# 24 of the 32 V groups as two 64-row halves added by GpSimd, four attention A pieces moved into the loop, a new loop order

## The chip, the cores and the metric

One core of a Trainium2 chip. The time is the device time of one execution in microseconds (us); the kernel before took a median of 1776.0 us in three runs (1775.54 to 1776.98). The engines are TensorE (PE; its weight loads stand apart as PEld), VectorE (DVE), ScalarE (ACT), GpSimd (POOL) and SyncE (SP), which issues nearly all DMAs.

## What is computed

Two attentions of 32 heads of 20 over 2048 positions, side by side in the output:

```python
# A: each position sees 8 positions, 2 apart, ending at itself
logits = einsum("bhsd,bhswd->bhsw", q, kg) * scale      # kg, vg: gathered k and v
o_a = einsum("bhsw,bhswd->bhsd", softmax(where(mask, logits, -1e9)), vg)
# B: full attention
p = softmax(einsum("bhqd,bhkd->bhqk", q, k) * Dh**-0.5)
o_b = einsum("bhqk,bhkd->bhqd", p, v)
return concatenate([o_a @ wo_a, o_b @ wo_b], axis=-1)   # q, k, v from x @ wqkv, each its own
```

All in fp32. The projections split both operands in a high and a low part (type fp32r) and add three products: high x high, high x low, low x high (`PASSES`).

## The kernel before

**Stages.** First attention A's projections, then B's q and k (both stored in memory). Then the *V stage*, B's v. Then the *loop*: B's attention in 512 steps (488 in the loop, the last 24 in a tail), with A's attention on GpSimd beside it. Then the rest of the output.

**A V group** (`v_group`, L854) makes 128 positions x 320 columns of v: 15 matmuls (five chunks of 128 of the contraction, three products each; `rows15`, L250) that add up in one PSUM bank, `ww` the weights' tiles and `xn`, `xl` those of x. ACT copies the bank into `ve`, one of four tiles (`ones`) that already hold a one beside each head, and SP stores `ve` in `vb_d`. Of 32 groups 30 run in the V stage, two in the loop's first steps. Banks come from four that rotate (`bank`, `give`).

**Score sets in the V stage.** B's softmax needs row maxima before its exponentials. A set (`b_max`, L687) is four matmuls of 60 rows x 512 columns (`bk`, `bq`): two pairs, one of a pair on rows 0 to 63 and the other on rows 64 to 127 of the array, into two adjacent banks, then one DVE maximum over both banks (`mx`). The sets run 24 steps ahead of the loop (`LEAD`): after each V group from the seventh on, one set.

**Order.** Every engine runs its instructions in program order (`InOrder`). `after(n, ...)` puts something n ticks later, `tick()` ends one; a V group is a tick, a loop step is a tick. After groups 8 and 16, x is loaded and split again (ACT takes the high part, GpSimd subtracts, `x_pieces(xb, ..., gp)`).

**Attention A** is 128 pieces (`a_attention`, `a_unit`): a piece loads two tiles of k or v (`akv`), multiplies by q (`aq`) or by the probabilities (`al`), and adds up, all on GpSimd. Twelve pieces run beside B's q and k, four in the V stage (after groups 18, 24, 27 and 30), the others in the loop, where `begin` hands them out by an estimate of GpSimd's time.

**The loop's order** is written out in the string `ORDER` (L944). S is two score halves (half of a step's 62-row matmul on 64 array rows) and their exponentials on ACT; M and N are two halves of the row maxima, M with one DVE maximum over two banks, N with two over one bank each; Y is one half of each kind; V begins the next step with its product with v; F is an output group of A; j is one DVE transpose for A; the digits are PSUM banks.

Of the kernel before, what the change touches and what calls it, by code (L numbers as in the profile page):

```python
# [10 lines left out]
F32 = mybir.dt.float32  # L11
# [8 lines left out]
DH = 20  # L20
# [50 lines left out]
def attention_pair(ctx, tc, xa, wqk_a, wv_a, wo_a, xb, wqk_b, wv_b, wo_b, oa, ob):  # L71
# [104 lines left out]
    def chunk(t, xi, k):  # L176
        return t[k // (KC - 1)][:, xi, k % (KC - 1)]
# [739 lines left out]
    def begin(i):  # L917
# [32 lines left out]
        "Y07M5M2S41F0Y71M5S42Y03V7S42M5Y01VY24Y35S06N17V2S03M4Y16VY70S15M3Y26V7S05jS14jM2VjM5S01Y23V4jY05M6S31VN05M2M6"  # L950
        "S14jF0Y15S42M6Y03V1Y24M6S05VY02M3S57Y61V0Y72M3S56VY71M5S24Y30V1S27M5Y43VS07Y62N54N31F0Y72S36Y54N01V7Y62N34S05V"
        "Y06S51Y23N74V0S13M5Y72VS13N74Y56N20F1Y72S36M4Y01V7Y62M4S03VY06M1S35S74N60V3Y72S16M4VY70M1S64S35N07V6Y41S02Y53V"
        "M0S72Y34V5Y06S71N42VY07M3S61Y25V7Y60S14N32VY06S15M3Y27V6Y01M3S52VS70M1M3M5F7Y04S31Y25N76V0Y15N43S72VY71S26Y54"
        "N03V7S64M1Y05VS64S03jN21jY57jF6jjY70M1S35Y46V7Y05M1S34VY03M5S41S72N30V4Y57S36M1VY07M5S31S42N70V3Y41M5S72VY70M1"
        "S46Y35V0Y74S16M2VY71M4S63Y20V7Y61M4S32VY06M2S14S75N60V1Y72S36M4VS07M2S64N51V0S72Y36M4VS76M2S10M4S76Y32V1Y07M4"
        "S26VY07S23M4S61N70V2Y36S75Y14VM6S05Y43V1Y02S76N53VY07S24M5S31N70V2Y36M4S71VY07Y16M4M2Y70F1Y72S36M4Y01V7Y62M4"
        "S03VY06M1S35Y74V0Y35M1S76VS73Y45S62N10V7M3S51Y06VM3S52Y16V0jY75M3S26VjY71M5S24Y30V1Y27M5S43VY07M3jM5jS21jF0Y71"
        "M3S25Y06V7Y51M3S02VY06M1S53Y74V0Y35M1S76VY73M4S62Y10V7Y62M4S31VY06M2S14S75N60V1Y72S36M4VY07M2S64S51N70V6Y52M3"
        "S71VY70Y15S24M6S03N15V2S07Y64Y31VM4S07Y61V3Y02M4S71VS07Y62M4S13V0Y72S64N15VY71M2S46S50N17V4Y35S62M0VY73Y26M0M4"
        "Y37F2Y01S36M4Y72V0Y13M4S76VY71M2S64S05N17V6Y04M2S51VY70N15Y42S36V0Y17M3S56VY71S26M3Y50V1Y27S63M4VjS07jM2M4Y61"  # L960
        "F0jjjY72S13M4Y06V7Y13M4S02VS06M2S14N75V0S16M2Y74VS15M6S23N04V1Y27M5S03VS07M2Y46S51V0S72M3Y56VY71M3S25Y60Y17V2"
        "Y36M4S01VY07Y16M4S32Y70V1Y26M4S73VY07M2S64S51N70V6Y52M3S71VY70M1S53S46N07V5Y41M2S06VY70Y61M2S45S07V6M4Y31S02V"
        "S75M3S02N16V7Y05S41M2VY06M4Y13S72Y60V1S72M4Y36VY07M4M2S61F0Y71M2Y46S05V7Y04M2S15VY06M4S13Y72Y60V1Y75M3S26VY07"
        "M5S24Y31V0jS72jM5S43jVjM1S74Y56V3jY70M1S46VY07M4S61M2Y70F6Y70S15M2Y46V7Y05S13Y24VM0S63Y45V2Y01M6S35VY01M3S75"
        "Y62V0Y17M3S56VY75M1Y63S04V5Y67M1S04VY07M3S62S15N70V6Y14M2S75VY70M4S13S26N07V1Y25M3S06VY07M5S24S31N70V2Y36M4S71"
        "VY07S16N35S42N70V1S36M4Y72VS03M4M6Y21F0Y72S36M4Y01V7Y62M4S03VY06M1S35S74N60V3S72M5S41VY07M5S42V1Y07S34M5VY07"
        "S23M5Y41V7Y02M5S34VY03M1S46S57N30V4Y51M2S76VY70M5S13S42N07V1S63M4Y02VY73S04M5jY21jF7jjjY06S51M3Y72V0Y16M3S75V"
        "Y71M5S24S03N17V2Y06S15M3VY07M5S14Y32V7Y01M5S43VY04M1S35Y67V0Y53M1S46VS73M4S62N01V7S63M4Y02VS31Y06M4S72Y36V1Y07"
        "M4S26VY07M2S46Y51V7Y04M2S65VY06M4S13Y27Y60V1Y25M3S76VS07M5S24Y31V0Y72M5S41VY74M2S16S50N47V1Y26M4S03VY07M2S64"
        "S51N70V6Y52M3S71VY70M1S53S46N07V5S41M2Y06VY74M2M0S65F7Y62S35M0Y74V6Y53M0S72VY75M3S20Y16V7Y05M3S21VjS06jM1M3S57"  # L970
        "jF0jjY71S26M3Y05V7Y61M3S02VY06M1S53S74N60V5Y71S62M3VY07M1S63Y45V0Y76M1S34VY73M5S42Y10V7Y24M5S31VY04M2S15S76N40"
        "V1Y72S35N46VY07S25M3S61N07V2S36M4Y01VS73S04M5N12V7M5S03Y41VY02S36Y54N71V0S26M3Y75VS61M3S72Y05V6Y71M3S52VY70M1"
        "S53S46N07V5Y41M2S06VY70S61M2M4Y07F6Y70M2S14Y56V7Y04M2S15VY06M4S13Y72Y60V1Y75S24N36VY07S25M3Y61V7Y02M3S56VY05"
        "S61M3Y27V5Y60M3S12VS07M1S63jM4jF0jjjY71M4S63Y02V7Y61M4S03VY06M1S35Y74V0Y35M1S76VY73M4S62Y10V3Y76M4S21VY07M1S64"
        "Y53V0Y74M1S56VY73M4S62S01N37V6Y05M3S21VY70M1S53S46N07V5Y41M2S06VY70Y61M2S45Y07V6Y51M2S04VY70M4S13S26N07V1Y25M3"
        "S06VS07M5Y24S31V0S72M5Y43VM1S75S64N30V7Y61S52M3VY06M1S53S47N60V5Y41S23M6VY04M1S37M5N40F3Y72S16M4Y03V7Y62M4S01V"
        "Y06M2S14S75N60V1Y72S63M4VY07M2S64S51N70V6Y52M3S71VY70M1S53Y46V7Y05M1S34VjS06jM3M1S57jF0jjY71S26M3Y05V7Y61M3S02"
        "VS06M1S53Y74V0M1S65Y43VY71M5S23V4Y70S12M5VY70M1S36S54N70V3S21M5Y47VY02S14M5S73N02V1S74M5Y03VY72S06M4S31N72V0"
# [12 lines left out]
        "jjY71S26M3Y05V7Y61M3S02VY06M1S53Y74V0Y35M1S76VY73M4S62Y10V3Y76M4S21VY07M1S64Y53V7Y60M1S45VY06M4S31S27N60V3S24"
        "Y15M6VY02M4S17S63N02V1S74M5Y03VS72jM5S04Y31jV7jY06M1S54VjM5S03S42N17jS06S53N14V2Y01M6S54VY03S15Y74N62V3Y40S15"
# [113 lines left out]
```

## Time and profile before

| | us |
|---|---|
| median of 3 runs | 1776.0 |
| the profiled execution | 1777.45 |
| its span, first to last instruction | 1775.6 |
| DVE, ACT, POOL busy in the span | 1337.9, 1323.5, 1209.8 |
| span of the 32 `ve` copies | 351.5 to 446.6 |

A row of a group of instructions reads: line, engine, operation, tile written<-tiles read, shapes, count | busy us, mean ns of one | idle time of the engine before them and what ended it. All work goes through one helper, so every row has L66, and the tiles' names tell the groups apart. A timeline row begins with its start and its length in us. Matmul durations are modelled and overlap, so starts are compared rather than lengths.

### The profile page before, as it was taken

What the parts mean: (1) busy time and instruction counts of PE and PEld (TensorE: products, weight loads), DVE (VectorE), ACT (ScalarE), POOL (GpSimd) and SP (SyncE); (2) the same over time, 40 slices, a digit from 0 to 9 for tenths busy, and PEclk for the clock granted to TensorE, in tenths of its full rate; (3) what the DMA queues carried; (4) which work ended last, traced back from release to release, by engine and by line L of the source; (5) the groups of instructions that cost most, each with busy time, mean ns of one, the idle gap of its engine ahead of it and who ended that gap; (6) DMA issues with size and microseconds to landing.
All of it is one profiled execution on the core that took longest, in us unless ns stands there. A gap on an engine that the chain in (4) does not pass through costs nothing.

```text
span 1775.6 us, 31540 instructions
## 1 busy us (share of the span) xinstructions
PE 1760.9 (99%) x11211; PEld 996.6 (56%) x11211; DVE 1337.9 (75%) x1805; ACT 1323.5 (75%) x2593; POOL 1209.8 (68%) x1072
## 2 busy tenths in 40 slices
PE   9999999999999999999999999999999999999999
PEld 7988888887444444444444444444444444444569
DVE  3100232268999999999999999999999999999300
ACT  4222322222998999989999999999999998999881
POOL 0000059227899999999999999899999962445241
PEclk9999999999999999999999999999999999999999
DMA  6333596854744544364436436353644422211123
GB/s 229 112 98 109 177 309 243 277 175 145 221 120 123 147 137 124 107 159 150 133 104 173 134 114 160 111 156 117 163 127 121 139 68 51 72 40 47 33 71 114
DMA packets 191190, 240.22 MB, mean 135 GB/s; under 512 B 89020, under 2 KB 115260, under 8 KB 190040
## 3 DMA queue, kind: packets, MB, share of 16 engines
q1 hardware_dynamic: 190456, 237.54, 45.0%
q8 instruction: 88, 1.44, 0.3%
q14 instruction: 70, 0.57, 0.1%
q10 hardware_dynamic: 576, 0.66, 0.1%
HBM read 173.21 MB, written 64.91 MB: 134 GB/s over the span
## 4 chain that ended last, share of the span: by engine, by line
PE 77%; POOL 13%; DVE 3%; issue 2%; DMA 2%; ACT 2%; SPq 1%; POOLq 0%; ACTq 0%; DVEq 0%
PE ps_st L66 77%; POOL akv L66 7%; DVE mx L66 3%; POOL braw L66 3%; POOL ao L66 1%; ACT e L66 1%; SPq L66 1%; DMA bq<-qb_d 1%; POOL al L66 1%; DMA stg<-wv_b 0%; POOL aot L66 0%; DMA stg<-xa 0%; ACT more L66 0%; DMA ot_b<-braw 0%; DMA rb<-s_d 0%
## 5 line engine op out<-in xcount | busy, mean ns | idle before, releaser
L66 DVE TENSOR_REDUCE mx<-ps_st 128x1 f32<-128x512 f32 (+1 forms) x1483 | 1214.6, 884 | 46.3 <-PE ps_st L66 41.4
L66 ACT ACTIVATE e<-ps_st 128x512 f32<-128x512 f32 x2048 | 1063.3, 616 | 32.9 <-PE ps_st L66 12.9
L66 PE MATMUL ps_st<-bq,bk 62*128 62x512 f32 x2048 | 560.9, 440 | 2.9 <-DMA bq<-mdr 1.6
L66 PE MATMUL ps_st<-e,vb 128*32 128x512 f32 x4096 | 544.6, 606 | 0.8
L66 PE MATMUL ps_st<-bk,bq 60*128 60x512 f32 x2048 | 539.4, 439 | 4.1 <-DVE mx L66 2.6
L66 PEld LDWEIGHTS ps_st<-bq,bk 62*128 62x128 f32 x2048 | 281.6, 184 | 449.8 <-ACT e L66 281.3
L66 POOL TENSOR_TENSOR braw<-braw,more 128x512 f32<-128x512 f32 x224 | 288.8, 1289 | 105.2 <-ACT more L66 104.7
L66 POOL TENSOR_TENSOR akv<-akv,aq 128x1280 f32<-128x1280 f32 x64 | 188.6, 2947 | 235.2 <-DMA akv<-ka_d 235.2
L66 PEld LDWEIGHTS ps_st<-bk,bq 60*128 60x128 f32 x2048 | 250.1, 184 | 83.4 <-DVE mx L66 46.9
L66 POOL TENSOR_TENSOR akv<-akv 128x640 f32<-128x640 f32 (+3 forms) x304 | 283.6, 933 | 14.7
L66 ACT COPY ro<-ps_st 128x320 f32<-128x320 f32 (+2 forms) x124 | 61.4, 497 | 223.3 <-PE ps_st L66 173.9
L66 PEld LDWEIGHTS ps_st<-e,vb 128*32 128x32 f32 x4096 | 82.2, 108 | 154.5 <-issue 72.4
L66 POOL TENSOR_TENSOR akv<-akv,al 128x1280 f32<-128x1280 f32 x64 | 152.2, 2378 | 0.2
L66 ACT COPY more<-ps_st 128x512 f32<-128x512 f32 x224 | 133.7, 597 | 3.7 <-PE ps_st L66 3.5
L66 PE MATMUL ps_st<-wc,xn 128*128 128x512 f32 (+1 forms) x576 | 133.5, 376 | 0.7 <-ACT xn L66 0.7
L66 PE MATMUL ps_st<-ww,xn 128*128 128x320 f32 x768 | 126.0, 314 | 0.0
L66 PEld LDWEIGHTS ps_st<-ww,xn 128*128 128x128 f32 x768 | 113.7, 188 | 21.0 <-ACT e L66 8.0
L66 PEld LDWEIGHTS ps_st<-wc,xn 128*128 128x128 f32 x576 | 106.2, 188 | 18.6 <-ACT xn L66 1.3
L66 PE MATMUL ps_st<-xn,w 128*128 128x512 f32 x480 | 115.8, 390 | 0.0
L66 PEld LDWEIGHTS ps_st<-xn,w 128*128 128x128 f32 x480 | 90.1, 188 | 19.3
L66 ACT CAST pr<-ps_st 128x512 fp32r<-128x512 f32 x40 | 23.6, 589 | 101.4 <-PE ps_st L66 101.4
L66 DVE TENSOR_TENSOR pr<-ps_st,pr 128x512 fp32r<-128x512 f32 x40 | 27.7, 691 | 91.0 <-ACT pr L66 88.3
(64 smaller groups left out, 992.1 us busy)
## 6 DMA issues: line engine op xcount, KB each, us to landing
akv<-ka_d SPq DMA_DIRECT2D x128, 320.0 KB
akv<-va_d SPq DMA_DIRECT2D x128, 320.0 KB
kb_d<-pr SPq DMA_DIRECT2D x20, 512.0 KB
qb_d<-pr SPq DMA_DIRECT2D x20, 512.0 KB
bk<-kb_d SPq DMA_DIRECT2D x16, 640.0 KB
bq<-qb_d SPq DMA_DIRECT2D x64, 160.0 KB
rb<-s_d SPq DMA_DIRECT2D x128, 64.0 KB
stg<-xb SPq DMA_DIRECT2D x12, 512.0 KB
```

The source lines that it names most:

```text
L66: return self.tc.keep_in_program_order(op(*a, **k))
```

## The change

Three edits.

1. `v_group` gets `halves`. With it each of the 15 matmuls becomes two: rows 0 to 63 of the contraction into one bank, rows 64 to 127 into a second. ACT copies both banks (the first into `ve`, the second into a tile `more`, three buffers), GpSimd adds `more` to `ve`, and the store of `ve` is issued one tick later. The main loop asks for it once six groups are done: 24 groups of the V stage. The first six, and the two in the loop, are as before.
2. The four A pieces of the V stage go: they come out of the loop's `begin` instead.
3. `ORDER` is made anew: 488 steps, 32 F and 80 j as before; S 661 (before 647), Y 630 (658), M 509 (517), N 152 (130). The last F stands at step 450 (before 434).

```diff
-    def v_group(n, half, s):
-        p = bank()
-        rows15(p, lambda xi, k: chunk(XB[n], xi, k)[:, s % 4 * 128:s % 4 * 128 + 128], WV[half])
+    def v_group(n, half, s, halves=False):
         ve = ones[s % 4]
-        act.copy(ve[:, :16 * VC].rearrange("p (h c) -> p h c", c=VC)[:, :, :DH],
-                 p[:, :320].rearrange("p (h d) -> p h d", d=DH))
-        give(p)
+        to = ve[:, :16 * VC].rearrange("p (h c) -> p h c", c=VC)[:, :, :DH]
+        ps2 = [bank() for _ in range(1 + halves)]
+        if halves:
+            for k in range(KC):
+                for i, (wi, xi) in enumerate(PASSES):
+                    for r, p in enumerate(ps2):
+                        rows = slice(r * HALF, r * HALF + HALF)
+                        pe.matmul(p[:, :320], chunk(XB[n], xi, k)[rows, s % 4 * 128:s % 4 * 128 + 128], WV[half][wi][rows, k],
+                                  start=(k == 0 and i == 0), stop=(k == KC - 1 and i == 2))
+        else:
+            rows15(ps2[0], lambda xi, k: chunk(XB[n], xi, k)[:, s % 4 * 128:s % 4 * 128 + 128], WV[half])
+        act.copy(to, ps2[0][:, :320].rearrange("p (h d) -> p h d", d=DH))
+        if halves:
+            more = sb.tile([128, 320], F32, tag="r", bufs=3, name="more")
+            act.copy(more, ps2[1][:, :320])
+            pool(to, to, more.rearrange("p (h d) -> p h d", d=DH), ALU.add)
+        for p in ps2:
+            give(p)
         c = 16 * VC + 11 * half
-        after(1, sp.dma_start, vb_d[s * 128:(s + 1) * 128, half * 16 * VC:half * 16 * VC + c], ve[:, :c])
+        after(1 + halves, sp.dma_start, vb_d[s * 128:(s + 1) * 128, half * 16 * VC:half * 16 * VC + c], ve[:, :c])
...
-        v_group(n, half, s)
+        v_group(n, half, s, groups > 5)
...
-        if groups > 16 and groups % 3 == 0 and groups != 21:
-            a_unit()
...
-        "Y07M1M3Y56V0Y71M3N25Y06V7Y04M2S15Y76V0Y15M2S74VY71M5S42S03Y17V4Y05S76M2VN05S71S62M3S07N51V6Y02S53N74VS05M1S73"
...
+        "Y07M1S36M4V0Y71M4M2Y06V7Y05M2S41Y76V0Y15M2S74VY71M5S42S03N17V4Y05S61M2VY07M5S13S42N70V1Y36M4S72VS07M2S64Y51V0"
...
```

On PE, in the V stage, before: a group (`ww` times `xn` and `xl`) and a score set (`bk` and `bq`) in turn; the set's matmuls are of 64 array rows or fewer, the group's of 128.

```order
277 L66 MATMUL ps_st<-ww,xn 128x320 x12
278 L66 MATMUL ps_st<-ww,xl 128x320 x3
279 L66 MATMUL ps_st<-bk,bq 128x512 x4
280 L66 MATMUL ps_st<-ww,xn 128x320 x12
281 L66 MATMUL ps_st<-ww,xl 128x320 x3
282 L66 MATMUL ps_st<-bk,bq 128x512 x4
```

And the same place after:

```order
277 L66 MATMUL ps_st<-ww,xn 128x320 x24
278 L66 MATMUL ps_st<-ww,xl 128x320 x6
279 L66 MATMUL ps_st<-bk,bq 128x512 x4
280 L66 MATMUL ps_st<-ww,xn 128x320 x24
281 L66 MATMUL ps_st<-ww,xl 128x320 x6
282 L66 MATMUL ps_st<-bk,bq 128x512 x4
```

A group has 30 matmuls for 15, all of 64 rows, between the same score sets. (The shapes here are those of the output: partitions x columns.)

On POOL, in the V stage, before: the split of x (`xn`, `xl`), a whole A piece (`akv`, `al`), the next split, and the two halves of the row maxima (`mtr`).

```order
82 L66 TENSOR_TENSOR xn<-stg,xn 128x1024 x2
83 L66 TENSOR_TENSOR xl<-stg,xl 128x512
84 L66 TENSOR_TENSOR akv<-akv,aq 128x1280
85 L66 TENSOR_TENSOR akv<-akv 128x2x320
86 L66 TENSOR_TENSOR akv<-akv 128x2x160
87 L66 TENSOR_TENSOR akv<-akv 128x2x64
88 L66 TENSOR_TENSOR akv<-akv 128x2x32
89 L66 TENSOR_TENSOR al<-akv 128x64
90 L66 TENSOR_TENSOR xn<-stg,xn 128x1024 x2
91 L66 TENSOR_TENSOR xl<-stg,xl 128x512
92 L66 CAST mtr<-mtr 128x32
93 L66 TENSOR_TENSOR mtr<-mtr 128x32
```

And after, from the same place to the first A piece:

```order
82 L66 TENSOR_TENSOR ve<-ve,more 128x16x20 x7
83 L66 TENSOR_TENSOR xn<-stg,xn 128x1024 x2
84 L66 TENSOR_TENSOR xl<-stg,xl 128x512
85 L66 TENSOR_TENSOR ve<-ve,more 128x16x20 x8
86 L66 TENSOR_TENSOR xn<-stg,xn 128x1024 x2
87 L66 TENSOR_TENSOR xl<-stg,xl 128x512
88 L66 TENSOR_TENSOR ve<-ve,more 128x16x20 x2
89 L66 CAST mtr<-mtr 128x32
90 L66 TENSOR_TENSOR mtr<-mtr 128x32
91 L66 TENSOR_TENSOR ve<-ve,more 128x16x20 x7
92 L66 TENSOR_TENSOR akv<-akv,aq 128x1280
```

The 24 adds stand before and behind the two splits, and the A pieces of this stage are gone; the next one comes behind the last add.

More of the change, by code (lines that the diff above doesn't have):

```diff
@@ L950, in attention_pair @@
[L950 to L954, printed above, removed]
@@ L1000, in attention_pair @@
[L1000 to L1001 removed]
+        "Y07M1S36M4V0Y71M4M2Y06V7Y05M2S41Y76V0Y15M2S74VY71M5S42S03N17V4Y05S61M2VY07M5S13S42N70V1Y36M4S72VS07M2S64Y51V0"
+        "M2S76Y14VjM2S75S46M0V7jS52jY34M0VS26M4S30Y71V2jY36M4jS01VY07S63Y45M1N70S65V3Y42M6S51VY02M4S17S63N20V1Y74M5S23V"
+        "Y07M2Y46S51Y70V4Y53M1S76VY07M5S31S42N70V3Y41M5S72VY70M1S46S35N07V4Y36M1S05VY07M5S31S42N70V3S41M5S72VM0S74Y56V2"
@@ new lines, in attention_pair @@
+        "Y07M2S46S51N70V4Y35M6S21VY05M1S37N64N50F3Y74M1S56Y03V7Y64S52M0VY63M4S20S71Y36V2M4S07N16VS05Y74Y31V2Y04M5S71V"
+        "Y70S34M5Y12V7S03N64Y51VjS06jM4M2S17F0jjjY71S26M4Y03V7Y62M4S01VY06M2S14Y75V0Y16M2S74VY71M5S42S30N17V4Y35S62M0V"
+        "Y73M5S20Y14V7S03M5Y21VY03S24M5Y17V0Y24M5S13VY74M1S36S05N47V3Y02S41M5VY70M1S46S35N07V4Y36M1S05VY07Y63S52M0S74"
+        "N63V5S70M1Y64VS70M1Y36S45V7M1S03Y46VY05S13Y24N67V0S13M4Y62VS71M4Y63N20F7Y61S02M4Y73V6Y02M4S71VY70M2S14S56N07V1"
+        "Y25S04N36VY07S25M3S61N07V2S36M4Y01VY73M4S06Y12V7Y06M4S31VY06M2S14Y75V6Y04M2S17VY05S71jM2jS46jN50jF7jY06S51M2"
@@ new lines, in attention_pair @@
+        "Y74V0Y15M2S76VS71M4S63N02V7S61M4Y03VS62M0S54N73V6S50Y12Y74VM2S01Y45V7Y60M2S15VY06M4S31S27N60V3Y24M5S71VY70M1"
+        "S46S35N07V4Y36M1S05VY07M5S31S42N70V3Y41M5S72VY70M1S46S35N07V4Y36M1S05VY07M5S31S42V7M0Y63S45VM0S26S34N57V2Y30"
+        "S16N54VY70M5Y13N42F0Y71M5Y43S02V7Y04M5S12VY04M1S35Y76V0Y53M1S74VY73M5S42S01N37V4Y05S36M1VY07M5S31S42N70V3S41j"
+        "M5Y72VS04jY71M5M2F0jjY71S26M4Y03V7Y62M4S01VY06M2S14S75N60V1Y72S36M4jVS07M2S64Y51V0M6S23Y41VY73S26M4S10N37V2Y16"
+        "M4S30VY73M0S64Y52V7Y63M0S45VY62M3S50Y17V2Y65M3S01VY07M5S14S32N70V1S36M4Y72VY03S74M5S21N03V7S62Y54M0VY62S35N40"
@@ new lines, in attention_pair @@
+        "N71S62V3S04M5Y72VS04M5Y71N23F0Y71M5Y42S03V7S01M5S43VM0S26Y54V3Y70M1S46VY07S45M1S63N70V4Y51M6S32VM0S25M6S34Y20"
+        "Y15V3Y42M6S01VY02S14M6Y53V2Y01M6S45VjS01jM4M6S32jF0jjY71M4S63Y02V7Y61M4S03VY06M1S35S74N60V3Y72M5S41VY70M1S46"
+        "S35N07V4Y36M1S05VY07M5S31S42N70V3S41M5S72VM0S74Y56V2Y73M0S46VY73M4S06S12N37V0Y16M4S32VY71M2S64Y05V7Y64M2S01V"
+        "Y06M4S13S27N60V1Y25M3S76VY07M5S24S31N70V2Y36S75Y14VM6Y05S43V1Y02S76M4VN07M2M4S61F0Y71S62M4Y03V7Y62M4S01VY06M2"
+        "S14S75N60V1Y72S36M4VY07M2S64S51N70V6Y52M3S71VS70M1S53N46V7S05M1Y34VS05Y63M1Y74V0S35jM1Y76VS53S74jM1N06F5jjjY07"
@@ new lines, in attention_pair @@
+        "S42S03N17V4Y05S61M2VY07M5S13Y42Y70V1Y63M4S27VS06M2S74N51V0M2S76Y45VY71S62M3S50N71V6S52M3Y70VY51S72M3Y06V5Y71M3"
+        "S02VY07M1S63Y45V0Y76M1S34VY73M5S42S01N37V4Y05S36M1VY07M5S31S42N70V3Y41M5S72VY70M1S46S35N07V4Y36M1S05VY07M5S31"
+        "S42N70V3Y41M5S72VS70M1S46Y53V7N04S12Y63VY02S14M5S37N20V1Y63M4S27VY06M2S74S15N60V7Y14M2S65VY06M4Y13S72Y60V1Y72"
+        "M4S36VY07M2S64S51N70V6Y52M3S71VY70M1S53S46N07V5Y41M2S06VY70Y61S42Y35N07V6Y52N14S03VS70Y15S23N64V7M0Y65S42VM0"
+        "S63M4S27")
```

86 lines of the change are left out of this document (35 added, 51 removed).

## The prediction

> **What bounds the kernel now.** I read the page first, then a table of stretches, then the timeline of the stretch that the change edits.
>
> ```profile
> span 1775.6 us, 31540 instructions
> PE 1760.9 (99%) x11211; PEld 996.6 (56%) x11211; DVE 1337.9 (75%) x1805; ACT 1323.5 (75%) x2593; POOL 1209.8 (68%) x1072
> ```
>
> PE is never idle by this line, but matmuls are pipelined and counted to their modelled ends, so the share says little. The table of stretches (busy time of PE, PEld, DVE, ACT, POOL; clock; DMA) separates the stages: the V stage with its score sets, the loop with attention A in it, the loop without it, the tail.
>
> ```profile
> 366.40:437.30 70.90, 70.90 (x440) 57.99 (x441) 54.90 (x49) 15.77 (x32) 37.83 (x32) 1.00 0.52 158
> 448.00:1400.00 952.00, 947.29 (x6504) 426.04 (x6497) 932.41 (x1284) 889.21 (x1761) 916.94 (x802) 1.00 0.48 137
> 1400.00:1645.00 245.00, 244.42 (x1680) 107.28 (x1678) 239.60 (x327) 231.33 (x455) 125.30 (x114) 1.00 0.25 67
> 1645.00:1776.00 131.00, 125.84 (x852) 90.06 (x850) 17.73 (x26) 79.37 (x162) 37.14 (x35) 0.97 0.24 74
> ```
>
> In the loop DVE is busy 98% (932 of 952, 240 of 245): its row maxima set the pace. POOL is 96% busy to 1400 us and 51% after it. In the V stage DVE has 16 us to spare, ACT 55 and POOL 33. There the chain of waits, in order of time, stays on PE after one wait for a load:
>
> ```profile
> 357.14 9.22 DMA bq<-qb_d
> 366.40 70.89 PE ps_st L66 x419
> ```
>
> So 366.4 to 437.3 us is PE's own time; the loop follows, to about 1645. The timeline shows what it is spent on: first two V groups back to back (before the score sets start), then one period of a score set and a group.
>
> ```profile
> 353.51 1.92 PE L66 MATMUL ps_st<-ww,xn 128*128 128x320 f32 x12
> 355.26 0.60 PE L66 MATMUL ps_st<-ww,xl 128*128 128x320 f32 x3
> 355.70 1.92 PE L66 MATMUL ps_st<-ww,xn 128*128 128x320 f32 x12
> ...
> 378.63 0.30 PEld L66 LDWEIGHTS ps_st<-bk,bq 60*128 60x128 f32 x4 [0.19 <-DVE mx L66]
> 378.63 0.73 PE L66 MATMUL ps_st<-bk,bq 60*128 60x512 f32 x4
> 379.17 2.36 DVE L66 TENSOR_REDUCE mx<-ps_st 128x2 f32<-128x1024 f32 x2 [0.70 <-PE ps_st L66]
> 379.29 2.03 PE L66 MATMUL ps_st<-ww,xn 128*128 128x320 f32 x12
> 381.16 0.60 PE L66 MATMUL ps_st<-ww,xl 128*128 128x320 f32 x3
> 381.69 0.30 PEld L66 LDWEIGHTS ps_st<-bk,bq 60*128 60x128 f32 x4 [0.19 <-DVE mx L66]
> ```
>
> Back to back a group takes 355.70 - 353.51 = 2.19 us, 0.146 us per matmul. In the alternation the group takes 381.69 - 379.29 = 2.40, the score set 379.29 - 378.63 = 0.66, the period 3.06 us. DVE's two maxima (2.36) fit inside. What a score set costs among other 60- and 62-row matmuls, the timeline of the loop's start shows: pairs that follow each other in that shape.
>
> ```profile
> 446.76 0.39 PE L66 MATMUL ps_st<-bk,bq 60*128 60x512 f32 x2
> 446.99 0.40 PE L66 MATMUL ps_st<-bq,bk 62*128 62x512 f32 x2
> 447.23 0.40 PE L66 MATMUL ps_st<-bk,bq 60*128 60x512 f32 x1
> 447.23 0.38 PE L66 MATMUL ps_st<-bq,bk 62*128 62x512 f32 x1
> ```
>
> A pair, one matmul on rows 0 to 63 and one on rows 64 to 127, goes every 0.23 to 0.24 us: the two run at once. Two pairs are 0.46 us, where the alternation pays 0.66. So each period loses 3.06 - 2.19 - 0.46 = 0.41 us at its two changes between 128-row and 64-row matmuls.
>
> **The change part by part.** *Matmuls.* A halved group is 30 matmuls of 64 rows in 15 pairs, in the shape of the score sets on either side, so both changes of shape go. No row has a 64-row matmul of 320 columns. The nearest: 0.146 for the whole matmul of 320 columns, and the pair of 512 columns scaled, 0.23 x 320 / 512 = 0.144. The dear bound is a pair whose weight load is not hidden; it is a rival below. I take 0.146, the row with the right column count: 15 x 0.146 + 0.46 = 2.65 us. From the first score set at 366.4 to the last, 23 groups with 23 sets lie between; 23 x (3.06 - 2.65) = **-9.4 us**. The first halved group and the 24th set lie outside (the group ends in the wait for `bq` that ends at 366.40 anyway). The Trainium skill (TensorE: Matmul & The Clock Gate, "Measured speedup vs the span model") gives each further tile of a pack about 4 ns; by that estimate a pair is 0.150, the period 2.71 and this term -8.1; no run here shows the 4 ns for this shape, and the scaled row lies below it.
>
> *Banks and ACT.* A group takes two of the four rotating banks, so a bank returns after two groups instead of four, behind two ACT copies (0.43 each) instead of one. In the steady period that is nothing: 0.86 us of copies against 2.65. But the first copies run late, as this timeline of ACT shows:
>
> ```profile
> 367.01 0.43 ACT L66 COPY ve<-ps_st 128x320 f32<-128x320 f32 x1 [1.83 <-DMA vb_d<-ve]
> 369.92 0.43 ACT L66 COPY ve<-ps_st 128x320 f32<-128x320 f32 x1 [2.48 <-DMA vb_d<-ve]
> 372.47 0.43 ACT L66 COPY ve<-ps_st 128x320 f32<-128x320 f32 x1 [2.13 <-DMA vb_d<-ve]
> 375.49 0.43 ACT L66 COPY ve<-ps_st 128x320 f32<-128x320 f32 x1 [2.59 <-DMA vb_d<-ve]
> ```
>
> These are the copies of groups 5 to 8 (counted from 0); each waits until the store of the same `ve` tile four groups earlier has landed. With four banks of slack PE did not notice. Now group 7's second bank is free at 367.44 instead of being ready at 366.9 (0.6 late), group 8's after 369.92 + 0.86 = 370.8 where PE arrives at 370.2 (0.6), group 10's at 376.4 against 376.2 (0.3). **+1.5 us**; ends 0 (the loads before them land sooner) and 4 (each of the four late copies in full).
>
> *GpSimd and SP.* POOL's rows of the V stage, and one of ACT's (groups of instructions, 366.3 to 437.3 us: busy, mean ns of one, idle before):
>
> ```profile
> L66 POOL TENSOR_TENSOR akv<-akv,aq 128x1280 f32<-128x1280 f32 x4 | 11.8, 2947 | 0.0
> L66 POOL TENSOR_TENSOR xn<-stg,xn 128x1024 fp32r<-128x1024 f32 x4 | 9.5, 2398 | 73.7 <-ACT xn L66 73.7
> L66 POOL TENSOR_TENSOR akv<-akv 128x640 f32<-128x640 f32 x4 | 6.3, 1566 | 0.3
> L66 POOL TENSOR_TENSOR akv<-akv 128x320 f32<-128x320 f32 x3 | 2.6, 871 | 0.2
> L66 POOL TENSOR_TENSOR xl<-stg,xl 128x512 fp32r<-128x512 f32 x2 | 2.6, 1288 | 0.0
> L66 POOL TENSOR_TENSOR akv<-akv 128x128 f32<-128x128 f32 x3 | 1.4, 460 | 0.2
> L66 POOL TENSOR_TENSOR akv<-akv 128x64 f32<-128x64 f32 x3 | 1.0, 322 | 0.2
> L66 POOL TENSOR_TENSOR al<-akv 128x64 f32<-128x64 f32 x3 | 1.0, 321 | 0.2
> ...
> L66 ACT CAST xn<-stg 128x1024 fp32r<-128x1024 f32 x4 | 4.0, 1051 | 0.0
> ```
>
> An add of 128x320 costs 0.87; 24 are 21 us, with the 12 us of splitting x 33 of some 63 us. Behind each add waits SP with the group's store, and behind that store, in SP's order, the second reload of x and the row maxima's way through memory; both are needed two groups or more later. The tight place is the split of x: 2 x 2.40 + 1.29 = 6.1 us in a row, behind an ACT cast of 1.05 and the two copies of the group before it (0.86). It ends 8.0 us after that group's matmuls, the add behind it at 8.9; the `more` buffer that this add holds is wanted by the group four further on, at 4 x 2.65 = 10.6. 1.7 us are to spare, so I cost it at nothing; were POOL later than that, ACT and then PE would stop for the difference.
>
> The four A pieces were 2.95 + 1.57 + 0.87 + 0.46 + 0.32 + 0.32 = 6.5 us of POOL each; 26 us go into the loop, with eight loads (two to a piece) in SP's queue there. POOL has 35 us free before 1400 and 120 after. The last output group of A moves from step 434 to 450 of 488. Nothing, as long as DVE sets the pace.
>
> *The loop.* Work per step is as before, 1952 score halves of each kind and 32 output groups. But the new order has 509 wide maxima for 517 and 934 single ones for 918; a reciprocal of A's softmax comes into the loop too.
>
> ```profile
> L66 DVE TENSOR_REDUCE mx<-ps_st 128x2 f32<-128x1024 f32 x506 | 612.0, 1213 | 3.7 <-PE ps_st L66 3.1
> L66 DVE TENSOR_REDUCE mx<-ps_st 128x1 f32<-128x512 f32 x906 | 584.6, 680 | 18.3 <-PE ps_st L66 14.1
> L66 DVE RECIPROCAL am<-am 128x32 f32<-128x32 f32 x14 | 4.7, 338 | 0.0
> ```
>
> By busy time per piece (584.6 / 906 = 0.645, 612.0 / 506 = 1.209) this is 16 x 0.645 - 8 x 1.209 + 0.34 = **+1.0 us** on the engine that sets the pace. DVE's waits of 22 us (3.7 + 18.3) are what another order can change: by a quarter either way, +-5 us, and I have no row for the sign.
>
> Sum: -9.4 + 1.5 + 1.0 = -6.9 us. The profiled execution took 1777.45 us, its span 1775.6 and 1.85 around it; 1777.45 - 6.9 = 1770.55. It lies 1.45 above the median of 1776.0, and measured runs are compared with that median, so the forecast is 1776.0 - 6.9 = **1769.1 us**.
>
> **The rivals.** *Weight loads one behind the other (slower).* At 512 columns a pair every 0.23 us would also hide two loads in turn, so the pair rows do not settle it for 320. The Trainium skill (TensorE: Matmul & The Clock Gate, "LDWEIGHTS") says that a load takes the time of its columns, not its rows: estimated from its formula 107 ns for 128 columns, so half a matrix loads no faster. As a mechanism here, with the page's row of one such load:
>
> ```profile
> L66 PEld LDWEIGHTS ps_st<-bk,bq 60*128 60x128 f32 x2048 | 250.1, 184 | 83.4 <-DVE mx L66 46.9
> ```
>
> The four loads of a score set above take 0.30 us, so the last begins 0.30 - 0.184 = 0.116 after the first: the spacing of two loads on the same rows. If the two halves queued, a group would be 30 x 0.116 = 3.5 us, the period 3.5 + 0.46 = 3.96, and the stage 23 x 0.90 = 20.7 longer: 1776.0 + 20.7 + 1.0 = 1798 us. It decides once a pair exceeds (3.06 - 0.46) / 15 = 0.173. Against it: four loads in turn would take 3 x 0.116 + 0.184 = 0.53, and the row says 0.30, two at once.
>
> *POOL paces the loop (slower).* If the 26 us of A pieces met a POOL that already set the pace, the loop would grow by up to 26: 1769.1 + 26 = 1795 us. For it: 96% busy to 1400. Against it: DVE is busier, and with POOL half idle after 1400 the share of DVE stays 98%. It decides when POOL's free 35 us are used up.
>
> *Eaten.* The loop's new order adds some 5 us of DVE waits, or the adds behind the split of x stop PE twice for 2 to 3 us: 1774 to 1776, no change.
>
> *More.* The new order saves 5 us of those waits: 1764.
>
> *The change doesn't do what it says:* if PE did not run the halves at once, the group would take 30 x 0.146; the pairs of the loop speak against that, and the price is beyond the first rival's. I give it no chance of its own.
>
> **How the numbers follow.** Forecast 0.62, more 0.10, eaten 0.14, loads in turn 0.07, POOL 0.07. About 0.2%, 3.6 us, is what a measurement of this kernel can tell from no change; faster therefore means below 1772.4. The forecast's own spread (early copies 0 to 4 us, loop a few) puts 0.03 of its 0.62 above that. Faster: 0.59 + 0.10 = 0.69; same: 0.14 + 0.03 = 0.17; slower: 0.14. The range goes from 1763 (the "more" case less 1) to 1777 (the "eaten" case plus 1) and leaves out the two slower rivals, 0.14, and the edges.
>
> **What would show it.** Right: the score sets of the V stage come every 2.65 us, the chain stays on PE, the stage after 366.4 ends near 429.5; the halved group's matmuls start in pairs 0.146 apart; PE waits for ACT copies only in the first four periods; the loop keeps its 1645 - 437 = 1208 us to within 5. Wrong: pairs over 0.17 apart (loads), ACT waiting for GpSimd adds or for stores of `ve` after 380 us, a loop over 1213 us with DVE under 97%, or POOL busy over 97% well beyond 1450 us.

## The result, and the profile after

The changed kernel takes 1767.18 us (median of 6 runs, 1766.22 to 1769.83), the kernel before beside it 1776.78 (6 runs, 1775.54 to 1778.18): a ratio of 0.9949, with its interval 0.9937 to 0.9962, or 9.6 us less. The forecast was 1769.1 in a range of 1763 to 1777. The profiled execution of the changed kernel took 1766.22 us against 1777.45 of the one before, so the two traces differ by 11.2 us, a little more than the medians.

The page of the changed kernel, span and busy times:

```profile
span 1764.4 us, 32352 instructions
PE 1751.5 (99%) x11571; PEld 996.1 (56%) x11571; DVE 1336.5 (76%) x1813; ACT 1330.0 (75%) x2617; POOL 1228.0 (70%) x1096
```

PE has 360 matmuls more (24 x 15) and is still counted 99%: the share tells nothing, as before. POOL has 18 us more, close to its 24 adds. The chain of waits through the V stage:

```profile
360.28 5.49 DMA vb_d<-ve
365.88 0.43 ACT ve L66
...
366.35 62.63 PE ps_st L66 x766
```

The stretch that was 70.89 us of PE is 62.63, and it now begins behind a store of `ve` and an ACT copy rather than behind the load of `bq`. One steady period of PE, a score set and a halved group, and the next set:

```profile
379.91 0.67 PE L66 MATMUL ps_st<-bk,bq 60*128 60x512 f32 x4
380.41 1.94 PE L66 MATMUL ps_st<-ww,xn 64*128 64x320 f32 x24
382.18 0.61 PE L66 MATMUL ps_st<-ww,xl 64*128 64x320 f32 x6
382.62 0.65 PE L66 MATMUL ps_st<-bk,bq 60*128 60x512 f32 x4
```

By starts: the set 0.50, the group 2.21 (0.147 a pair), the period 2.71. From the first full set (365.24) to the 24th (428.56) it was 63.32 us where the kernel before took 366.40 to 436.77, 70.37. The table of stretches shows the rest, with the columns of the one before:

```profile
448.00:1400.00 952.00, 949.24 (x6520) 423.57 (x6516) 937.74 (x1298) 890.45 (x1764) 921.13 (x809) 1.00 0.47 136
1400.00:1645.00 245.00, 242.38 (x1662) 107.19 (x1662) 237.12 (x324) 228.56 (x451) 144.04 (x128) 1.00 0.26 72
```

DVE is still busy 98% (937.74 of 952) and 97%; POOL took over the A pieces (144 us for 125 in the second row), in its idle time. The two changes of pace that the forecast had not seen lie at the two ends of the loop. Three stretches, each with the granted clock as the third number from the right: the loop's first steps after the change, the loop's last steps before it, and the same steps after it:

```profile
431.00:435.50 4.50, 4.33 (x19) 3.83 (x17) 3.23 (x4) 1.08 (x2) 4.34 (x3) 0.63 0.11 39
```

```profile
1656.50:1664.00 7.50, 6.93 (x29) 2.70 (x30) 1.68 (x4) 5.21 (x10) 1.93 (x4) 0.54 0.12 35
```

```profile
1650.00:1656.00 6.00, 6.00 (x46) 3.56 (x47) 0.00 (x0) 5.10 (x11) 2.89 (x4) 1.00 0.14 47
```

Inside both drops the granted clock is 0.50 (432.2 to 435.4 us after the change, 1657 to 1663 us before it). So a mean of 0.63 over 4.5 us is 3.3 us at half clock (4.5 x 0.37 / 0.5), and one of 0.54 over 7.5 us is 6.9 us. In these two executions the kernel before lost its clock at the end of the loop; the changed kernel ran the same steps at full clock, and lost some at the loop's start.

Where the time went, step by step, from the starts of PE's products with v (PV):

| us | before | after | difference so far |
|---|---|---|---|
| first full score set of the V stage | 366.40 | 365.24 | -1.2 |
| the 24th set | 436.77 | 428.56 | -8.2 |
| first PV of the loop | 447.7 | 440.5 | -7.1 |
| PV of step 480 | 1640.6 | 1633.8 | -6.8 |
| PV of step 488 (the tail begins) | 1666.9 | 1655.7 | -11.2 |
| end of the span | 1775.6 | 1764.4 | -11.2 |

So in these two executions the V stage gave 8.2 us, the loop's start took 1.1 back, 480 steps another 0.4, the last eight steps of the loop gave 4.4, and the tail nothing. The loss at the start is the dropped clock of this execution: from the 24th set to the first PV takes 12.0 us here and 10.9 before, but 10.4 in the six traces below that have the new order and no drop there.

### The profile page after: what moved, and what is told of

The parts are those of the page before. It is cut to its first block, busy times and chain, and to the rows that moved or that the text cites. A ratio compares the mean times of both kernels' runs of the same rounds, so it can differ in the third digit from the quotient of the medians.

```text
span 1764.4 us, 32352 instructions
## 1 busy us (share of the span) xinstructions
PE 1751.5 (99%) x11571; PEld 996.1 (56%) x11571; DVE 1336.5 (76%) x1813; ACT 1330.0 (75%) x2617; POOL 1228.0 (70%) x1096
## 4 chain that ended last, share of the span: by engine, by line
PE 88%; POOL 6%; DMA 2%; DVE 1%; ACT 1%; issue 1%; SPq 0%; POOLq 0%; ACTq 0%; DVEq 0%
PE ps_st L66 88%; POOL akv L66 3%; POOL braw L66 1%; DVE mx L66 1%; ACT e L66 1%; DMA bk<-kb_d 1%; POOL ww L66 1%; SPq L66 0%; DMA stg<-wo_a 0%; DMA vb_d<-ve 0%; POOL aot L66 0%; POOL al L66 0%; DMA s_d<-braw 0%; DMA akv<-ka_d 0%; DMA qb_d<-pr 0%
## 5 line engine op out<-in xcount | busy, mean ns | idle before, releaser
L66 PE MATMUL ps_st<-bq,bk 62*128 62x512 f32 x2048 | 552.7, 439 | 2.7 <-DVE mx L66 1.2
L66 PE MATMUL ps_st<-bk,bq 60*128 60x512 f32 x2048 | 532.5, 438 | 3.0 <-DVE mx L66 2.0
L66 PEld LDWEIGHTS ps_st<-bq,bk 62*128 62x128 f32 x2048 | 277.4, 184 | 446.3 <-ACT e L66 285.5
L66 ACT COPY more<-ps_st 128x512 f32<-128x512 f32 (+1 forms) x248 | 144.5, 583 | 2.3 <-PE ps_st L66 1.5
L66 PE MATMUL ps_st<-ww,xn 64*128 64x320 f32 (+1 forms) x1056 | 125.8, 311 | 0.4 <-ACT ve L66 0.4
L66 PEld LDWEIGHTS ps_st<-ww,xn 64*128 64x128 f32 (+1 forms) x1056 | 116.8, 187 | 14.1 <-ACT e L66 8.0
```

What stands on the lines that cost most here:

```text
L66: return self.tc.keep_in_program_order(op(*a, **k))
```

## The experiments

**Whole groups.** The new order and the moved pieces without the halves.

```diff
-        v_group(n, half, s, groups > 5)
+        v_group(n, half, s)
```

> The changed kernel with all V groups whole (128-row matmuls, one bank, no add); the four A pieces stay in the loop and the new order stays. Theory (the halves are the gain: they take away two changes of array shape per period): the V stage's period goes back from 2.70 to 3.06 us, 23 periods cost 8.3, and the 1.2 us of early waits for banks go; the time rises by about 7 us over the changed kernel, to some 1774. Rival (the new order or the moved pieces are the gain): the time stays within 2 us of the changed kernel, at 1767.

Measured: 1774.27 us (11 runs) against 1777.16, ratio 0.9981 (0.9972 to 0.999). PE in the V stage:

```profile
394.62 0.73 PE L66 MATMUL ps_st<-bk,bq 60*128 60x512 f32 x4
395.28 2.03 PE L66 MATMUL ps_st<-ww,xn 128*128 128x320 f32 x12
397.14 0.60 PE L66 MATMUL ps_st<-ww,xl 128*128 128x320 f32 x3
397.68 0.74 PE L66 MATMUL ps_st<-bk,bq 60*128 60x512 f32 x4
```

The period is 3.06 again. The loop is that of the changed kernel: the eight steps from 480 to 488 take 21.9 us in both, 26.3 before. So the halves, given the rest, are worth 1774.27 - 1767.18 = 7.1 us; the other edits together 2.9. By the two ratios, each against the kernel before that ran beside it, it is 5.7 and 3.4, so such differences hold to about 1.5 us; the V stage of the traces gives 7.1 for the halves.

**Only the ends halved.** The first and the last of the 15 matmuls in two halves, the 13 between whole. Where the set and the group meet, both sides are now of 64 rows; the change of shape has moved inside the group.

```diff
+                    if not (first or last):
+                        pe.matmul(ps2[0][:, :320], x, w, start=False, stop=False)
+                        continue
...
+                        pe.matmul(p[:, :320], x[rows], w[rows], start=first, stop=last)
```

> The changed kernel with only the first and the last of the 15 matmuls of each of the 24 groups in halves (64 rows, two banks), the 13 between whole. The score sets now have neighbours of their own shape, but the array changes shape twice inside the group. Theory (each change of shape costs, wherever it is): the period is 3.0 to 3.1 us as with whole groups, 1773 to 1775. Rival (the loss was the wait and the unhidden weight load where a group and a set meet): 2.65 to 2.75 us, 1766 to 1768.

Measured: 1774.2 us (12 runs), ratio 0.998 (0.997 to 0.9991), as with whole groups. One period:

```profile
391.30 2.13 PE L66 MATMUL ps_st<-ww,xn 64*128 64x320 f32 x13
...
393.91 0.63 PE L66 MATMUL ps_st<-bk,bq 60*128 60x512 f32 x4
394.37 2.13 PE L66 MATMUL ps_st<-ww,xn 64*128 64x320 f32 x13
```

The set itself is down to 0.46, but the period is 3.07: the 0.41 us went into the group. The cost belongs to the change between 128 and 64 rows wherever it stands, 0.2 us each, and not to what lies between a group and a set (banks, the wait for DVE). The Trainium skill (TensorEngine Tiling (Array Packing), "Key Properties") says that a change of tiling mode drains TensorE; it gives no figure. The rows agree that a change costs something, and put it at 0.2 us here.

**Halves apart.** The 15 upper halves first, then the 15 lower ones.

```diff
-            for k in range(KC):
-                for i, (wi, xi) in enumerate(PASSES):
-                    for r, p in enumerate(ps2):
+            for r, p in enumerate(ps2):
+                for k in range(KC):
+                    for i, (wi, xi) in enumerate(PASSES):
```

> The changed kernel with the 15 upper halves of a group first and the 15 lower halves after them, so that no two neighbours are a pair. Theory (two halves run at once only when they stand next to each other, since matmuls begin in order): the group takes 30 x 0.146 = 4.4 us, the period 4.9, and 23 periods cost 50 us: about 1817. Rival (halves of one row group each are in themselves twice as short, or the engine runs ahead to the other rows): the period stays at 2.70, 1767.

Measured: 1795.8 us in one run, against 1777.43. The period is 3.91 us, not 4.9. PE in the middle of a group, where the program has `xl` of the upper halves three times and then `xn` of the lower ones:

```profile
395.24 0.30 PE L66 MATMUL ps_st<-ww,xl 64*128 64x320 f32 x1
395.35 0.30 PE L66 MATMUL ps_st<-ww,xn 64*128 64x320 f32 x1
395.39 0.30 PE L66 MATMUL ps_st<-ww,xl 64*128 64x320 f32 x1
395.50 0.30 PE L66 MATMUL ps_st<-ww,xn 64*128 64x320 f32 x1
395.54 0.31 PE L66 MATMUL ps_st<-ww,xl 64*128 64x320 f32 x1
```

The three `xl` are 0.15 us apart: one row half alone goes no faster than whole matmuls, so without a partner the group costs twice. That was expected. What was not: the lower halves' `xn` starts at 395.35, ahead of the upper halves' `xl` at 395.39 and 395.54, which come before it in the program. About three matmuls at each of the two seams run beside those of the other half; the second seam has the score set in it, whose first upper-half matmul starts at 392.92, ahead of a lower-half `xl` of the group before it at 393.06. Together that is an estimated 6 x 0.147 = 0.9 us, near the 1.0 between 4.9 and 3.91. So "Every engine runs its instructions in program order", as the part on the kernel before has it, does not hold on TensorE between different row halves. The Trainium skill (TensorE: Matmul & The Clock Gate, "The mechanism") says that matmuls start and end in program order; these rows differ, for starts on different row halves, and the measurement decides.

**Only the halves.** The old order, and the four A pieces left in the V stage.

```diff
+        if groups > 16 and groups % 3 == 0 and groups != 21:
+            a_unit()
...
-        "Y07M1S36M4V0Y71M4M2Y06V7Y05M2S41Y76V0Y15M2S74VY71M5S42S03N17V4Y05S61M2VY07M5S13S42N70V1Y36M4S72VS07M2S64Y51V0"
+        "Y07M1M3Y56V0Y71M3N25Y06V7Y04M2S15Y76V0Y15M2S74VY71M5S42S03Y17V4Y05S76M2VN05S71S62M3S07N51V6Y02S53N74VS05M1S73"
...
```

> The kernel before with the halves alone: four A pieces kept in the V stage, the old order kept. Theory: period 2.70 us in the V stage until the first piece, then GpSimd has 33 + 26 of some 62 us to do, adds wait behind pieces of 6.5 us, and PE stops for 0 to 2 us at each of the last three; 7 us gained less 0 to 4, 1770 to 1774. Rival (order and pieces are the gain): no gain, 1776 to 1777. The end of the loop is the old one here: if the drop of the clock at its end was a matter of the order, it is in this profile too.

Measured: 1777.05 us (11 runs), ratio 0.9996 (0.9987 to 1.0006): nothing. The V stage gained as in the changed kernel (period 2.70, 24th set at 430.39, first PV at 441.1), and the loop's first 32 steps gave it all back: 82.5 us, where the kernel before takes 74.3. The waits of that start (425 to 480 us: who waited for whom, us in total, times, the longest):

```profile
PE ps_st L66 <- DVE mx L66: 6.6, 3, 5.4
DVE turn L66 <- POOL ww L66: 5.9, 1, 5.9
```

GpSimd had the adds and the A pieces in the same stage and came into the loop late, and the first transposes of A on DVE (`turn`, the j of steps 8 to 12) waited for it. They did not wait for A's values, which were ready at 323 us. By the kernel's tags `turn` takes one of three buffers called `stg`, and the row names what held it: GpSimd's split of the output weights (`ww`), which reads those buffers and ended at 464.6 us. In the kernel before that split ended at 463.7, hardly sooner, but the loop had begun 6.6 us later (first PV at 447.7) and its transposes found the buffer free. Behind the transposes in DVE's order stood the row maxima, and PE waited for those. So the time is the rival's, but for a reason that neither side had named. The clock at the old loop's end did not drop in this trace: steps 480 to 488 took 23.6 us (26.3 before, with the drop).

**The pieces back.** The changed kernel with the four A pieces in the V stage again, and the new order kept.

```diff
+        if groups > 16 and groups % 3 == 0 and groups != 21:
+            a_unit()
```

> The changed kernel with the four A pieces put back into the V stage, halves and new order kept. Theory (GpSimd, with adds, splits and pieces, is then late when the loop begins, and DVE, which transposes for A, waits for it): the V stage ends at 429 to 431 us, the first 32 steps of the loop take 5 to 8 us more than 75, the time goes up by 5 to 8, to 1772 to 1775. Rival (what was lost with the halves alone was lost to the old order): 1766 to 1769.

Measured: 1780.21 us (11 runs), ratio 1.0013 (1.0005 to 1.0022), 13 us more than the changed kernel and more than expected. The V stage is the same (24th set at 429.03). The split of `ww` ended at 463.3 us, in the changed kernel at 455.2. The stretch 450 to 475 us, first with the pieces back, then in the changed kernel:

```profile
450.00:475.00 25.00, 20.22 (x118) 6.92 (x119) 15.72 (x24) 15.84 (x32) 24.52 (x22) 0.80 0.72 182
```

```profile
450.00:475.00 25.00, 25.00 (x174) 9.64 (x178) 24.65 (x37) 24.51 (x49) 24.29 (x26) 1.00 0.71 184
```

POOL is full in both. With the pieces back DVE loses 9 of its 25 us, and the granted clock of 0.80 adds 10 us at half speed. DVE's own timeline shows the wait:

```profile
463.35 0.31 DVE L66 STREAM_TRANSPOSE turn<-ao 128x128 f32<-128x128 f32 x1 [5.84 <-POOL ww L66]
```

The first 32 steps take 83.8 us for 75.0; the other 4.5 us of the loop's 13.3 (1206.6 for 1193.3) come later, and I did not find where the larger part of them arises. So the halves pay only with the pieces moved.

**The old order.** The pieces moved and the groups halved, with the old string.

```diff
-        "Y07M1S36M4V0Y71M4M2Y06V7Y05M2S41Y76V0Y15M2S74VY71M5S42S03N17V4Y05S61M2VY07M5S13S42N70V1Y36M4S72VS07M2S64Y51V0"
+        "Y07M1M3Y56V0Y71M3N25Y06V7Y04M2S15Y76V0Y15M2S74VY71M5S42S03Y17V4Y05S76M2VN05S71S62M3S07N51V6Y02S53N74VS05M1S73"
...
```

> The halves and the pieces left to the loop, with the old order string: its output groups of A then find their tiles ready later than planned and follow each other in bunches. Theory: the V stage is that of the changed kernel (429 us at its end), the loop pays for the bunches 0 to 6 us and has the old end (4 us): 1770 to 1778. Rival (the order is of no account): 1767 to 1769.

Measured: 1877.92 us (4 runs), ratio 1.0555 (1.0542 to 1.0569): a hundred more, missed by far. The V stage is that of the changed kernel (24th set at 429.87); the 480 steps of the loop take 1302 us for 1193. The stretch of the loop with A in it:

```profile
448.00:1400.00 952.00, 903.38 (x5960) 393.42 (x5962) 855.90 (x1173) 818.16 (x1614) 842.27 (x739) 0.97 0.44 125
```

DVE falls from 98% to 90% and the clock to 0.97. In this trace A's transposes of the second block find nothing to do at steps 19 to 24 (the pieces are not there yet) and come at 47 to 50; every later output group is a block late, and the two of a pair run within half a step (their copies at 87.7 and 88.1, 119.7 and 120.1) instead of some steps apart (83.8 and 91.8, 111.8 and 119.8 in the changed kernel). From 448 to 1645 us DVE's maxima wait 113 us for PE, where the changed kernel has 13.6. That the banks which the string assigns no longer fit what runs is the likely reason; no run shows it. Order and pieces are one edit here: moved without the order, the pieces cost a hundred us.

**The loop's last maxima late.** The changed kernel with two M of its last lines put at the very end of the string, so that the maxima run further behind the steps, as in the kernel before.

```diff
-        "M4S36VY07M2S64S51N70V6Y52M3S71VY70M1S53S46N07V5Y41M2S06VY70Y61S42Y35N07V6Y52N14S03VS70Y15S23N64V7M0Y65S42VM0"
-        "S63M4S27")
+        "M4S36VY07S64S51N70V6Y52S71VY70M1S53S46N07V5Y41M2S06VY70Y61S42Y35N07V6Y52N14S03VS70Y15S23N64V7M0Y65S42VM0"
+        "S63M4S27M2M0")
```

> The changed kernel with two M tokens (two wide maxima of DVE with their four matmuls) taken out of the order some ten steps before the loop's end and put behind its last token, so that maxima are as far behind at the end as in the old order. Theory (at the old end PE waited for the last maxima, and the clock that TensorE was granted dropped after it): 2 to 5 us more, 1769 to 1772, with a stretch of about half clock at the loop's end. Rival (the dropped clock was chance, the order's end of no account): 1767.

Measured: 1771.83 us (8 runs), ratio 0.9969 (0.9958 to 0.9979), 4.7 more than the changed kernel. Steps 480 to 488 take 27.2 us (21.9 in the changed kernel, 26.3 before), and the clock falls as it did in the trace of the kernel before:

```profile
1650.00:1657.00 7.00, 6.66 (x30) 2.69 (x30) 0.87 (x3) 4.72 (x9) 1.77 (x4) 0.56 0.06 15
```

So how far the maxima are behind when the string ends costs time at the loop's end (4.7 us by the medians, 3.6 by the ratios). Not all of the 4.4 us is there in each execution: with the old order and no drop ("Only the halves") the eight steps took 23.6 us, 1.7 more than the new end, and the other 2.7 of the kernel before came with the dropped clock.

**More of the same, in the tail.** There 24 output groups of B stand between 62-row score matmuls. Halved in the same way, with DVE copying and adding:

```diff
-        p = bank()
-        out_matmuls(p, qc, n, range(KC))
-        store_rows(p, out_dst(qc, n))
+        ps2 = [bank() for _ in range(2)]
...
+        dve.tensor_copy(o, ps2[0][:, :320])
+        dve.tensor_tensor(o, ps2[1][:, :320], o, ALU.add)
```

> The changed kernel with the 24 output groups of B behind the loop's end in halves too; DVE copies the first bank and adds the second (ACT copied before). Theory (a change of array shape costs 0.2 us wherever it is): between two score steps of the tail a group stands behind a product with v and ahead of scores; the change to the scores goes and their first pair is as quick as the others, 5.50 us for two steps become 5.0 to 5.2, eleven times: 3 to 5 us less, 1762 to 1764. Rival (ACT's exponentials set the tail's pace, or the two banks that a group takes make the scores wait): 1766 to 1770.

Measured: 1776.81 us (11 runs), ratio 1.0002 (0.9993 to 1.0011): the whole gain lost. A period of two steps in the tail, first in the changed kernel, then here:

```profile
1676.50 1.32 PE L66 MATMUL ps_st<-bq,bk 62*128 62x512 f32 x8
1677.74 1.92 PE L66 MATMUL ps_st<-e,vb 128*32 128x512 f32 x16
1679.60 2.03 PE L66 MATMUL ps_st<-ww,xn 128*128 128x320 f32 x12
...
1682.00 1.31 PE L66 MATMUL ps_st<-bq,bk 62*128 62x512 f32 x8
```

```profile
1652.41 1.92 PE L66 MATMUL ps_st<-e,vb 128*32 128x512 f32 x16
1654.27 2.03 PE L66 MATMUL ps_st<-ww,xn 64*128 64x320 f32 x24
...
1656.57 0.63 PE L66 MATMUL ps_st<-bq,bk 62*128 62x512 f32 x4
1657.39 1.35 PE L66 MATMUL ps_st<-bq,bk 62*128 62x512 f32 x4 [0.19 <-DVE ro L66]
1658.67 1.92 PE L66 MATMUL ps_st<-e,vb 128*32 128x512 f32 x16
```

The period goes from 5.50 to 6.26. The group takes 2.30 for 2.40, but it holds two banks until DVE's second operation on them, and the score matmuls behind it wait for a bank; they take 2.10 us for 1.24. There was also less to win than in the V stage: only one neighbour of the group is of 64 rows or fewer, and towards the PV products (128 rows) a change now stands where none of rows stood.

Two more kernels tried to make room: the group put ahead of the two PV products (and so behind the scores), with the halves and without.

```diff
-            b_pv(i - LAG - 1)
-            b_pv(i - LAG)
             if fill:
                 fill.pop(0)()
+            b_pv(i - LAG - 1)
+            b_pv(i - LAG)
```

> The tail's output groups of B in halves (as in the run before, DVE copies and adds), and moved ahead of the two products with v instead of behind them, so that a group's two banks are emptied while those products run. Theory (the halves in the tail failed for want of banks alone, and a change of shape costs 0.2 us there too): two steps take 5.0 to 5.2 us for 5.50, eleven times, 3 to 5 us less than the changed kernel, 1762 to 1764. Rival (the exponentials, now wanted sooner behind the scores, make PE wait): 1766 or more.

> The changed kernel with the tail's output groups moved ahead of the two products with v, whole and copied by ACT as before. Theory: the same number of changes of shape, so 5.4 to 5.6 us for two steps and 1766 to 1768; what the run beside it gains over this one is then the halves' own. Rival (the place is what counts): 1763.

Measured: 1774.94 us with halves (11 runs, ratio 0.9985, 0.9974 to 0.9996) and 1772.01 without (6 runs, 0.9961, 0.9946 to 0.9976); both miss, and both lie above the changed kernel. With halves there is a period of 6.07 with a group of 2.88 us:

```profile
1674.77 2.52 PE L66 MATMUL ps_st<-ww,xn 64*128 64x320 f32 x24
1675.25 1.76 PEld L66 LDWEIGHTS ps_st<-ww,xn 64*128 64x128 f32 x23 [0.31 <-ACT e L66]
...
1677.65 1.92 PE L66 MATMUL ps_st<-e,vb 128*32 128x512 f32 x16
...
1680.84 2.52 PE L66 MATMUL ps_st<-ww,xn 64*128 64x320 f32 x24
```

The second weight load of a group, the first for its second bank, starts only 0.49 us after the group does, behind ACT's exponentials of the scores just ahead of it: in this place a group no longer holds banks that scores want, but wants banks that ACT still reads. Whole groups in the same place give 5.7. No kernel of this study is faster than the changed one.

## Why the prediction was right, step by step

- *The period.* Predicted 2.65, measured 2.70: 23 x 0.36 = 8.3 us for 9.4. The group was right (2.21 for 2.19, 0.147 a pair for 0.146), the score set was not: 0.50 for 0.46. The term that was put at nothing is DVE: "DVE's two maxima (2.36) fit inside" was read from a period of 3.06. A set's second pair needs the two banks that the second maximum of the set before it reads. In the changed kernel:

```profile
380.35 2.36 DVE L66 TENSOR_REDUCE mx<-ps_st 128x2 f32<-128x1024 f32 x2 [0.34 <-PE ps_st L66]
382.47 0.48 PEld L66 LDWEIGHTS ps_st<-bk,bq 60*128 60x128 f32 x4
```

  The maximum ends at 382.71, and the second pair's two loads start at 382.77, 0.30 after the first pair's. With the ends alone halved the period is 3.06, the maximum is done before the set begins, and the four loads take 0.34 for 0.48 and the set 0.46, beside the same 64-row neighbours. The traces' own sum, from the set at 379.91: its second maximum ends 2.80 later, the next set's second loads start 0.06 after that, the next group 0.34 after those, and the set after it 2.19 later; 5.39 us for two periods, 2.70 each. So in most sets of this stage PE now waits a little for DVE (about 0.1 us, too short for the rows to name it). This is read from the traces; no run with quicker maxima was made. The Trainium skill's 4 ns for each further tile (TensorE: Matmul & The Clock Gate, "Measured speedup vs the span model") would by estimate make a period of 2.71, but by a pair of 0.150, and that is not where the time is: the pair took 0.147. That the halves are worth this was shown by putting the whole groups back (7.1 us), and that it is the change of shape, by halving the ends alone.
- *The early copies.* Predicted +1.5 at groups 7, 8 and 10 (0.6, 0.6, 0.3); measured +1.2 (the first periods were 3.28, 3.18, 2.66 and 2.85, so 0.58, 0.48, -0.04 and 0.15 over 2.70). PE's rows name the cause at the first of them:

```profile
366.35 2.02 PE L66 MATMUL ps_st<-ww,xn 64*128 64x320 f32 x23 [0.38 <-ACT ve L66]
```

  Together 8.3 - 1.2 = 7.1 us, the 70.37 - 63.32 of the traces. The further 1.2 us at the 24th set are the load of `bq`, which landed earlier in this execution; its time differs from one execution to the next (the first matmul of the first set starts anywhere from 363.97 to 365.75 in the traces of this study), and it is no part of the change that I can show.
- *GpSimd beside the V stage.* Costed at nothing, with the split of x as the tight place. These rows are POOL's:

```profile
383.64 0.82 POOL L66 TENSOR_TENSOR ve<-ve,more 128x320 f32<-128x320 f32 x1 [0.81 <-ACT more L66]
384.59 4.78 POOL L66 TENSOR_TENSOR xn<-stg,xn 128x1024 fp32r<-128x1024 f32 x2
389.32 1.30 POOL L66 TENSOR_TENSOR xl<-stg,xl 128x512 fp32r<-128x512 f32 x1
390.57 2.36 POOL L66 TENSOR_TENSOR ve<-ve,more 128x320 f32<-128x320 f32 x3
```

  An add took 0.82 (0.87 from another row), three queue up behind the split and are done at 392.9, and PE's matmul rows show no wait from 380 to 428.5 us, so the cover held. ACT waited for a store of `ve` once more after 380 us (3.0 us at 381.2), which I had named as a sign against me; it did not reach PE.
- *The moved pieces.* Costed at nothing, and the loop did take them: 480 steps went from 1192.9 to 1193.3 us, so "POOL paces the loop" is out. But I treated the move as a side of the change that costs nothing, and the runs show it to be a condition; that the change contained it was luck as far as the forecast goes. Left in the V stage, the pieces cost 13 us with the new order, and with the old one they take the whole gain. I had looked for GpSimd's limit inside the V stage, where 33 of 63 us were used; it lay at the stage's end, where the loop's first transposes wait for a buffer that it still reads.
- *The loop.* +1.0 predicted from eight wide maxima turned to 16 single ones and a reciprocal. The groups of DVE from 448 to 1645 us, before and after, have all maxima in one row:

```profile
L66 DVE TENSOR_REDUCE mx<-ps_st 128x1 f32<-128x512 f32 (+1 forms) x1412 | 1138.2, 871 | 22.0 <-PE ps_st L66 17.2
```

```profile
L66 DVE TENSOR_REDUCE mx<-ps_st 128x1 f32<-128x512 f32 (+1 forms) x1422 | 1140.3, 869 | 18.3 <-PE ps_st L66 13.6
```

  These windows hold slightly different steps. Over the same 480 steps (447.7 to 1640.6 us before, 440.5 to 1633.8 after) the maxima's busy time grew by 3.1 us (1135.2 to 1138.3), the waits before them fell by 3.8 (22.1 to 18.3), and the steps grew by 0.4. "+-5, no row for the sign" held a term that could have been read: the last eight steps. Before the change they run while PE waits for maxima and then at half clock. The new string ends with the maxima less far behind, and in the traced executions that is 4.4 us, which the forecast's sum lacks; putting two of them back at the end restored the loss (4.7 us). Of the 4.4, 1.7 are there without a drop of the clock and 2.7 came with it. At the loop's other end 3.3 us at half clock cost about 1.6 in the traced execution (12.0 for 10.4). By medians all edits but the halves gave 2.5 to 2.9, less than the 4.4; how often either drop comes is open.
- *The rivals.* Loads one behind the other: out, the pairs came every 0.147 us, under the 0.173 from which it decides. "Eaten": not what happened, but just what the halves alone do. "More" is nearest to the miss of 2.7 us between the forecast's 6.9 and the measured 9.6, but not by its mechanism: the waits that it would save fell by 3.8 and were used up by longer maxima, and what came, came at the order's end. Two misses of opposite sign stand in the 2.7: the V stage gave 7.1 for 7.9, and the rest gave 2.5 where it was to cost 1.0. That the total lies so near is in part luck.

## What to carry to other kernels

Where matmuls of 128 rows alternate with matmuls of 64, count the changes: here 0.2 us each, saved by cutting the large ones into row halves, as long as the second bank and the extra evacuation have room on engines that are off the path; in the tail the same cut saved 0.1 us a period and its banks cost 0.86. Then ask which engine is next: here DVE's maxima, which fitted inside the old period, hold the new one at 2.70. An edit that frees time on one engine by loading another has to be followed to the first instruction that waits for the loaded engine, which here stood a stage later. And when an order is made anew, read its start and its end apart from its middle: 480 steps moved by 0.4 us, the last eight by 4.4 (2.7 of it with a clock that does not drop in every execution).

## What the runs showed of the hardware

- TensorE runs matmuls of different row halves beside each other even when they are not neighbours in the program, here about three ahead (starts out of program order, 395.35 before 395.39 and 395.54; a period of 3.91 where 4.9 was expected).
- The clock can be lost without a long wait of TensorE, and the waits ahead of the drop do not decide it: before the drop in the changed kernel they were 0.80 and 0.17 us, as these rows show.

```profile
430.29 0.73 PE L66 MATMUL ps_st<-bk,bq 60*128 60x512 f32 x3 [0.80 <-DVE mx L66]
...
431.42 0.51 PE L66 MATMUL ps_st<-bk,bq 60*128 60x512 f32 x2 [0.17 <-DVE mx L66]
431.85 3.35 PE L66 MATMUL ps_st<-ww,xn 128*128 128x320 f32 x12
435.00 0.85 PE L66 MATMUL ps_st<-ww,xl 128*128 128x320 f32 x3
```

  The 12 matmuls behind them took 3.15 us by their starts, where 12 such at full clock take 1.86 (395.28 to 397.14, above). The drops last 3.3, 6.9 and 10 us by the quoted rows. The Trainium skill (TensorE: Matmul & The Clock Gate, "What's actually happening") has the clock halved after an idle window of about 3.4 us. The lengths agree with multiples of that, but these rows show no wait near 3.4 us ahead of the drop. The same two waits (0.79 to 1.08 and 0.16 to 0.40 us) stand at this place in all twelve traces, and a drop follows in three: the changed kernel, the whole groups and the old order. What decides is open.
